# Moving turned q, k and x across partitions by DMA, for 64x64 tensor tiles in a fused attention and FFN kernel

## The chip, the cores and the metric

The kernel runs on one core of one Trainium2 chip. The metric is device time in microseconds (us) of one execution. Every kernel here was timed beside the kernel before on the same chip; most executions of the kernel before agree within 0.3%. A "fast" run is one no more than 1.5% above the fastest run of the same kernel; only fast runs enter a ratio. A ratio is the mean time of one kernel's fast runs over that of the other's of the same rounds, so it is not quite the ratio of the medians that are quoted.

Engine names in the profile: PE is TensorE (PEld its weight loads), DVE VectorE, ACT ScalarE, POOL GpSimd (here it only issues loads), SP SyncE (in the kernel before it only issues stores and two small loads at the start).

## The reference

Chunked attention over 64-token chunks, then an FFN without a nonlinearity:

```python
# q, k, v: (8, 8, 576, 64) float32
q_c = q.reshape(B, H, nc, 64, D)              # same for k, v
scores = scale * q_c @ k_c^T                  # 64 x 64 for each chunk and head
attn = softmax(scores)
out = attn @ v_c
x = out.transpose(0, 2, 1, 3).reshape(4608, 512)
return ((x @ w1) * (x @ w2)) @ w3 @ w_out     # d_ff = 1024
```

## The kernel before

Tokens are worked off in 18 "pairs" of 256 tokens (4 chunks). `ORDER` is a string that lists all steps in program order; each engine executes its own steps in that order. A letter is a step: T turns q or k of a pair (DVE transposes within blocks of 32x32), S scores, E exponential (ACT), P values, N normalise, X turns the result x (DVE), A and B the two FFN products, C copies the first to SBUF (ACT), M multiplies (DVE), O the output product, Y its copy. V, W and Z fold w3 and w_out into one matrix early on.

A DVE transpose leaves the 64 rows of the head dimension as two parts in the *same* 32 partitions. So scores contract over 32 partitions twice, and values write 32-partition tiles, which x then needs for its own transpose (shortened, `...` marks a cut):

```python
def do_S(p):                       # 64 matmuls a pair on 32x64 tiles
    ...
    for h in range(H):
        for e in range(2):
            for i in range(NB):
                mm(s_t[p][half[i % 2], i // 2, h * CH:(h + 1) * CH],
                   lhsT=qkT[blk[i], 1, e, h, :], rhs=qkT[blk[i], 0, e, h, :],
                   start=(e == 0), stop=(e == 1))

def do_P(p, u):                    # 64 matmuls a pair on 64x32 tiles
    ...
    mm(pv[blk[g], r, at:at + W],
       lhsT=e[half[r], u, 2 * g + n, qh * BL:(qh + 1) * BL],
       rhs=vbuf[p % 7][half[r], u, 2 * g + n, 0:W], start=True, stop=True)

def mm_ab(p, j, which):            # FFN: tiles of 256 tokens
    ...
    for i in range(2):
        for ki in range(KO):
            mm(ps_t[p, j][:, which, i * PT:(i + 1) * PT],
               lhsT=w[:, ki, (2 * j + i) * P:(2 * j + i + 1) * P],
               rhs=xt[:, ki, p * PT:(p + 1) * PT], start=(ki == 0), stop=(ki == KO - 1))

def do_O(p):                       # last pair: three pieces of one PSUM tile
    ...
    for u, n0, n1, copy in (...):
        mm_o(p, u, n0, n1)
        copy(o_sb[:, u, n0:n1], t[:, u, n0:n1])
        store(p, u, u + 1, n0, n1, o_sb)
```

The loads of q, k and v cast float32 to bf16 and go through POOL's queue; only q and k of pair 0 come through SP's queue and are cast by ACT. There are four PSUM tiles of 2 x 512 float32 for everything.

The softmax here doesn't subtract the row's maximum and nothing guards it: scores larger than these inputs give would overflow.

Of the kernel before, what the change touches and what calls it, by code (L numbers as in the profile page):

```python
# [9 lines left out]
l0 q1 i0 k1 v1 i1 i2 l2 i3 l3 l4 o h0 h1 l5 D0.0.16.64 T0.0 T0.1 l6 S0 T1.0 E0 P0 D0.1.4.512 T1.1 l7  # L10
N0.0 S1 D1.0.5.512 X0.0 N0.1 X0.1 A0.0 E1 B0.0 C0.0 P1 M0.0 A0.1 N1.0 X1.0 B0.1 C0.1 N1.1 A0.2 X1.1
B0.2 C0.2 M0.1 A1.0 T2.0 B1.0 C1.0 M0.2 A1.1 T2.1 l8 B1.1 C1.1 M1.0 S2 M1.1 A0.3 E2 T3.0 B0.3 C0.3
P2 M0.3 A1.2 N2.0 X2.0 B1.2 C1.2 N2.1 A1.3 X2.1 B1.3 C1.3 M1.2 A2.0 T3.1 l9 B2.0 C2.0 M1.3 S3 T4.0
A2.1 E3 M2.0 B2.1 T4.1 C2.1 P3 l10 M2.1 A2.2 N3.0 B2.2 C2.2 X3.0 A2.3 N3.1 B2.3 X3.1 C2.3 M2.2 S4
M2.3 A3.0 E4 B3.0 C3.0 A3.1 M3.0 B3.1 C3.1 V0 A3.2 M3.1 B3.2 C3.2 V1 A3.3 M3.2 B3.3 C3.3 V2 W0 M3.3
V3 T5.0 W1 Z0 V4 V5 T5.1 W2 Z1 V6 V7 T6.0 P4 l11 Z2 S5 T6.1 W3 E5 N4.0 X4.0 N4.1 X4.1 T7.0 A4.0 Z3
B4.0 T7.1 C4.0 P5 l12 M4.0 S6 N5.0 O0 E6 X5.0 N5.1 X5.1 T8.0 O1 Y0 T8.1 P6 l13 Y1 S7 N6.0 O2 E7 X6.0
N6.1 X6.1 T9.0 T9.1 O3 Y2 A4.1 Y3 B4.1 C4.1 A4.2 M4.1 B4.2 C4.2 A4.3 M4.2 B4.3 C4.3 P7 l14 M4.3 S8
N7.0 O4 E8 X7.0 N7.1 X7.1 T10.0 A5.0 T10.1 Y4 B5.0 C5.0 A5.1 M5.0 B5.1 C5.1 A5.2 M5.1 B5.2 C5.2 A5.3
M5.2 B5.3 C5.3 A6.0 M5.3 B6.0 C6.0 P8 l15 M6.0 S9 N8.0 O5 E9 X8.0 N8.1 X8.1 T11.0 A6.1 T11.1 Y5 B6.1  # L20
C6.1 A6.2 M6.1 B6.2 C6.2 A6.3 M6.2 B6.3 C6.3 P9 l16 M6.3 S10 N9.0 O6 E10 X9.0 N9.1 X9.1 T12.0 A7.0
T12.1 Y6 B7.0 C7.0 A7.1 M7.0 B7.1 C7.1 A7.2 M7.1 B7.2 C7.2 A7.3 M7.2 B7.3 C7.3 P10 l17 M7.3 S11
N10.0 O7 E11 X10.0 N10.1 X10.1 T13.0 A8.0 T13.1 Y7 B8.0 C8.0 A8.1 M8.0 B8.1 C8.1 A8.2 M8.1 B8.2 C8.2
A8.3 M8.2 B8.3 C8.3 P11 M8.3 S12 N11.0 O8 E12 X11.0 N11.1 X11.1 T14.0 A9.0 T14.1 Y8 B9.0 C9.0 A9.1
M9.0 B9.1 C9.1 A9.2 M9.1 B9.2 C9.2 A9.3 M9.2 B9.3 C9.3 P12 M9.3 S13 N12.0 O9 E13 X12.0 N12.1 X12.1
T15.0 A10.0 T15.1 Y9 B10.0 C10.0 A10.1 M10.0 B10.1 C10.1 A10.2 M10.1 B10.2 C10.2 A10.3 M10.2 B10.3
C10.3 P13 M10.3 S14 N13.0 O10 E14 X13.0 N13.1 X13.1 T16.0 A11.0 T16.1 Y10 B11.0 C11.0 A11.1 M11.0
B11.1 C11.1 A11.2 M11.1 B11.2 C11.2 A11.3 M11.2 B11.3 C11.3 P14 M11.3 S15 N14.0 O11 E15 X14.0 N14.1
X14.1 T17.0 A12.0 T17.1 Y11 B12.0 C12.0 A12.1 M12.0 B12.1 C12.1 A12.2 M12.1 B12.2 C12.2 A12.3 M12.2
B12.3 C12.3 P15 M12.3 S16 N15.0 O12 E16 X15.0 N15.1 X15.1 A13.0 Y12 B13.0 C13.0 A13.1 M13.0 B13.1  # L30
C13.1 A13.2 M13.1 B13.2 C13.2 A13.3 M13.2 B13.3 C13.3 P16 M13.3 S17 N16.0 O13 E17 X16.0 N16.1 X16.1
A14.0 Y13 B14.0 C14.0 A14.1 M14.0 B14.1 C14.1 A14.2 M14.1 B14.2 C14.2 A14.3 M14.2 B14.3 C14.3 P17
M14.3 A15.0 N17.0 X17.0 B15.0 C15.0 N17.1 O14 X17.1 M15.0 A15.1 Y14 B15.1 C15.1 A15.2 M15.1 B15.2
C15.2 A15.3 M15.2 B15.3 C15.3 A16.0 M15.3 B16.0 C16.0 O15 M16.0 A16.1 Y15 B16.1 C16.1 A16.2 M16.1
B16.2 C16.2 A16.3 M16.2 B16.3 C16.3 A17.0 M16.3 B17.0 C17.0 O16 M17.0 A17.1 Y16 B17.1 C17.1 A17.2
M17.1 B17.2 C17.2 A17.3 M17.2 B17.3 C17.3 M17.3 O17 Y17
# [4 lines left out]
def kernel(  # L41
# [24 lines left out]
    PT = 2 * UT  # L66
    NP = NT // PT
# [35 lines left out]
    xt = wpool.tile([P, KO, NT], bf, name="xt")  # L103
# [3 lines left out]
    vbuf = [consts.tile([P, 2, H, VW], bf, name=f"vbuf{i}") for i in range(7)]  # L107
# [16 lines left out]
    def load_qk(p, which=(0, 1)):  # L124
        if p not in qk_t:
            qk_t[p] = io.tile([P, 2, H, 2 * D], bf, tag="qk", bufs=6, name="qk")
        for s in which:
            if p == 0:

                raw = io.tile([P, H, 2 * D], f32, tag="raw", name="raw")  # L130
                inorder(nc.sync.dma_start(
                    raw[:], (q, k)[s][0, :, 0:4 * CH, :].rearrange("h (p t) d -> p h (t d)", t=2)))
                inorder(nc.scalar.copy(qk_t[p][:, s], raw[:]))  # L133
                continue
            for at, b, c, m in spans(4 * p, 4):
                load(qk_t[p][at * BL:(at + m) * BL, s],
                     (q, k)[s][b, :, c * CH:(c + m) * CH, :].rearrange("h (p t) d -> p h (t d)", t=2))

    def load_v(p):
        for u in range(2):  # L140
            for at, b, c, m in spans(4 * p + 2 * u, 2):
                load(vbuf[p % 7][at * CH:(at + m) * CH, u, :, 0:D],
                     v[b, :, c * CH:(c + m) * CH, :].rearrange("h p d -> p h d"))
# [17 lines left out]
    qkT_t, s_t, e_t, pv_t, xn_t = {}, {}, {}, {}, {}  # L161

    def do_T(p, s):


        if s == 0:
            qkT_t[p] = asb.tile([P, 2, 2, H, CH], bf, tag="qkT", bufs=2, name="qkT")
        inorder(nc.vector.transpose(  # L168
            qkT_t[p][:, s].rearrange("p e h (y t) -> p h t e y", t=2),
            qk_t[p][:, s].rearrange("p h (t e y) -> p h t e y", t=2, e=2)))  # L170

    def do_S(p):
        qkT = qkT_t.pop(p)
        s_t[p] = s_t.pop(p) if p in s_t else psum("s_ps")
        for h in range(H):
            for e in range(2):
                for i in range(NB):
                    mm(s_t[p][half[i % 2], i // 2, h * CH:(h + 1) * CH],
                       lhsT=qkT[blk[i], 1, e, h, :],
                       rhs=qkT[blk[i], 0, e, h, :], start=(e == 0), stop=(e == 1))  # L180
# [7 lines left out]
    def do_P(p, u):  # L188
        e = e_t[p] if u == 0 else e_t.pop(p)
        pv = pv_t[p, u] = psum("pv")  # L190
        for n in range(2):
            for qh in range(2):
                for g in range(NB):
                    for r in range(2):
                        at = (2 * qh + n) * W
                        mm(pv[blk[g], r, at:at + W],
                           lhsT=e[half[r], u, 2 * g + n, qh * BL:(qh + 1) * BL],
                           rhs=vbuf[p % 7][half[r], u, 2 * g + n, 0:W], start=True, stop=True)

    def do_P2(p):  # L200
        do_P(p, 0)
        do_P(p, 1)

    def do_N(p, u):
# [3 lines left out]
        xn_t[p, u] = asb.tile([P, 2, 4, D], bf, tag="xn", bufs=2, name="xn")  # L208
        inorder(nc.vector.tensor_mul(xn_t[p, u][:], pv[:, :, :, 0:D], rc.to_broadcast([P, 2, 4, D])))  # L209

    def do_X(p, u):
        t0 = p * PT + u * UT
        inorder(nc.vector.transpose(  # L213
            xt[:, :, t0:t0 + UT].rearrange("p o (m y) -> p m o y", y=BL),
            xn_t.pop((p, u))[:].rearrange("p r (c n) (z o) -> p (r c) o n z", c=2, o=KO)))

    ab_t, ps_t, a_t = {}, {}, {}
# [9 lines left out]
    def mm_ab(p, j, which):  # L227
        w = (w1, w2)[which]
        for i in range(2):
            for ki in range(KO):  # L230
                mm(ps_t[p, j][:, which, i * PT:(i + 1) * PT],
                   lhsT=w[:, ki, (2 * j + i) * P:(2 * j + i + 1) * P],
                   rhs=xt[:, ki, p * PT:(p + 1) * PT], start=(ki == 0), stop=(ki == KO - 1))

    def do_A(p, j):
        ps_t[p, j] = ps_t.pop((p, j)) if (p, j) in ps_t else psum("ab_ps")
        mm_ab(p, j, 0)

    def do_B(p, j):
        mm_ab(p, j, 1)  # L240
# [5 lines left out]
    def do_M(p, j):  # L246
        if p not in ab_t:
            ab_t[p] = msb.tile([P, FO, PT], bf, tag="ab", bufs=7, name="ab")
        inorder(nc.vector.tensor_mul(  # L249
            ab_t[p][:, 2 * j:2 * j + 2, :].rearrange("p j t -> p (j t)"), a_t.pop((p, j))[:],  # L250
            ps_t.pop((p, j))[:, 1, :]))

    def store(p, u0, u1, n0, n1, o_sb):
        inorder(nc.sync.dma_start(
            out[p * PT + u0 * UT:p * PT + u1 * UT, n0:n1].rearrange("(u p) n -> p u n", p=UT),
            o_sb[:, u0:u1, n0:n1]))

    def mm_o(p, u, n0, n1):
        for ki in range(FO):
            mm(ps_t[p][:, u, n0:n1], lhsT=ab_t[p][:, ki, u * UT:(u + 1) * UT],  # L260
               rhs=w3o[:, ki, n0:n1], start=(ki == 0), stop=(ki == FO - 1))

    def do_O(p):
        ps_t[p] = psum("o_ps")
        if p < NP - 1:
            for u in range(2):
                mm_o(p, u, 0, DM)
            del ab_t[p]
            return

        t = ps_t[p]
        o_sb = msb.tile([P, 2, DM], f32, tag="o_sb", name="o_sb")
        for u, n0, n1, copy in ((0, 0, DM, nc.scalar.copy), (1, 0, DM // 2, nc.scalar.copy),
                                (1, DM // 2, DM, nc.vector.tensor_copy)):
            mm_o(p, u, n0, n1)
            inorder(copy(o_sb[:, u, n0:n1], t[:, u, n0:n1]))  # L276
            store(p, u, u + 1, n0, n1, o_sb)

    def do_Y(p):
# [4 lines left out]
        store(p, 0, 2, 0, DM, o_sb)  # L284
# [29 lines left out]
    def load_half3(i):  # L314
# [7 lines left out]
    do = {"l": load_pair, "q": lambda p: load_qk(p, (0,)), "k": lambda p: load_qk(p, (1,)), "v": load_v, "i": load_w12, "o": load_wo, "h": load_half3, "T": do_T, "S": do_S, "E": do_E,  # L322
          "P": do_P2, "N": do_N, "X": do_X, "A": do_A, "B": do_B, "C": do_C, "M": do_M, "D": do_D, "V": do_V,
# [33 lines left out]
```

## Time and profile before

The median is 254.5 us; the profiled span is 252.7 us.

| what | value | where it is read |
|---|---|---|
| PE busy | 93% of the span | page, part 1 |
| one pair in the middle (152.10 to 164.10) | 12.0 us | windows |
| one pair late, with no attention left | 10.44 us (224.91 to 235.35) | timeline |
| values and scores of a pair | 0.63 + 0.64 us for 128 matmuls | timeline |
| loads keep DMA full (9 tenths or more) | until about 126 us | page, part 2 |

The page: PE's busy time, then busy tenths in 40 slices of 6.3 us for PE, the granted clock, and the DMA engines.

```profile
PE 234.9 (93%) x3841; PEld 170.5 (67%) x3841; DVE 156.4 (62%) x233; ACT 86.3 (34%) x116; POOL 82.9 (33%) x110
...
PE   1389999999899999999999999999999999999993
...
PEclk9999999999999999999999999999999999999999
DMA  7999999999999999999953020202021120102022
```

PE reads 9 nearly everywhere after the start, and so does DMA for the first 20 slices. The next view gives the busy time of each engine in three stretches (us and instruction count for PE, PEld, DVE, ACT, POOL, then the granted clock, a DMA share that counts overlapping packets, and GB/s).

```profile
73.00:130.00 57.00, 56.47 (x989) 39.57 (x988) 36.46 (x55) 20.47 (x27) 29.16 (x38) 1.00 1.58 182
152.10:164.10 12.00, 11.87 (x210) 8.96 (x209) 8.14 (x12) 4.38 (x6) 0.00 (x0) 1.00 0.13 47
225.00:235.50 10.50, 10.50 (x82) 7.84 (x81) 2.75 (x4) 3.36 (x5) 0.00 (x0) 1.00 0.13 51
```

PE has no idle time to speak of in any of them. The timeline of PE in one pair (start, length, operation, shapes, count):

```profile
152.10 0.70 PE L88 MATMUL pv<-vbuf,e 64*32 64x65 bf16 x64
152.73 0.70 PE L88 MATMUL s_ps<-qkT 32*64 32x64 bf16 x64
153.57 3.61 PE L88 MATMUL o_ps<-w3o,ab 128*128 128x512 bf16 x16
```

Start to start, values take 0.63 us, and from scores to the output product 0.84. (Elsewhere in this trace, where FFN products follow scores, scores take 0.64, as at 37.90 us.) The next view is the chain of waits for the same moment (start, length, what):

```profile
152.21 0.59 ACT a_sb L244
...
152.83 0.70 DVE ab L249
...
153.57 3.61 PE o_ps L88 x16
```

The chain does not run through values and scores. It runs through the copy of the last FFN product (ACT, 0.59 us) and its multiplication (DVE, 0.70), and the output product starts 0.04 us after the latter. Values and scores fill just that hole.

### The profile page before, as it was taken

How to read it: one execution, taken by the hardware profiler on the slowest of the kernel's cores; microseconds unless marked ns; L12 is line 12 of the kernel's file. 1: busy time of each engine (PE TensorE's matmuls, PEld its weight loads, DVE VectorE, ACT ScalarE, POOL GpSimd, SP SyncE). 2: the span in 40 equal slices, each digit the busy share in tenths (PEclk: the TensorE clock that was granted, in tenths of full speed). 3: DMA queues.
4: the chain of work that ended last, by engine and by line, in shares of the span. 5: the costliest groups of instructions: out<-in, count | busy, mean ns of one | idle time of the engine just before them, and what ended most of it. 6: DMA issues, size and time to landing. Idle time of an engine off the chain costs nothing.

```text
span 252.7 us, 8382 instructions
## 1 busy us (share of the span) xinstructions
PE 234.9 (93%) x3841; PEld 170.5 (67%) x3841; DVE 156.4 (62%) x233; ACT 86.3 (34%) x116; POOL 82.9 (33%) x110
## 2 busy tenths in 40 slices
PE   1389999999899999999999999999999999999993
PEld 1237878854555577866868686868686868678662
DVE  1665999699996457486665758584945445432230
ACT  3312424432433343333334243343334332323321
POOL 8756975657984567654020000000000000000000
PEclk9999999999999999999999999999999999999999
DMA  7999999999999999999953020202021120102022
GB/s 177 182 184 177 182 175 202 196 184 167 175 170 214 244 227 182 199 167 148 187 38 92 3 83 4 86 3 86 5 81 44 46 81 5 64 22 84 0 86 83
DMA packets 89763, 29.90 MB, mean 118 GB/s; under 512 B 73728, under 2 KB 85248, under 8 KB 89728
## 3 DMA queue, kind: packets, MB, share of 16 engines
q0 software_dynamic: 82592, 18.88, 80.4%
q1 hardware_dynamic: 7136, 10.49, 11.8%
q8 instruction: 30, 0.49, 0.7%
q14 instruction: 5, 0.04, 0.0%
HBM read 38.80 MB, written 9.44 MB: 191 GB/s over the span
## 4 chain that ended last, share of the span: by engine, by line
PE 65%; DMA 14%; DVE 10%; POOL 4%; ACT 3%; issue 3%; DVEq 0%; POOLq 0%
PE ab_ps L88 39%; PE o_ps L88 25%; DMA w<-in_moe_w_dram 4%; DVE ab L249 4%; DMA qk<-in_q_dram 4%; DMA qk<-in_k_dram 3%; DVE w3T L290 3%; DMA vbuf<-in_v_dram 3%; ACT a_sb L244 3%; POOL w L91 1%; DVE qkT L168 1%; POOL vbuf L91 1%; POOL qk L91 1%; POOL wo L91 1%; DVE xt L213 1%
## 5 line engine op out<-in xcount | busy, mean ns | idle before, releaser
L88 PE MATMUL ab_ps<-xt,w 128*128 128x256 bf16 x1136 | 128.0, 273 | 1.3 <-DVE xt L213 1.3
L88 PEld LDWEIGHTS <-w 128*128 128x128 bf16 x1152 | 112.3, 98 | 19.4 <-DVE xt L213 2.4
L249 DVE TENSOR_TENSOR ab<-a_sb,ab_ps 128x512 bf16<-128x512 f32 x71 | 48.3, 682 | 71.6 <-ACT a_sb L244 71.6
L244 ACT COPY a_sb<-ab_ps 128x512 f32<-128x512 f32 x71 | 41.6, 586 | 79.3 <-PE ab_ps L88 79.3
L88 PE MATMUL o_ps<-w3o,ab 128*128 128x512 bf16 (+1 forms) x296 | 65.3, 373 | 2.7 <-ACT o_sb L276 1.1
L88 PEld LDWEIGHTS <-ab 128*128 128x128 bf16 x296 | 28.7, 97 | 33.3 <-issue 1.6
L168 DVE STREAM_TRANSPOSE qkT<-qk 128x1024 bf16<-128x1024 bf16 x36 | 45.1, 1287 | 8.5 <-ACT qk L133 5.1
L91 POOL DMA_DIRECT2D vbuf<-in_v_dram x40 | 33.9, 852 | 31.3 <-PE pv L88 16.3
L283 ACT COPY o_sb<-o_ps 128x1024 f32<-128x1024 f32 x17 | 17.2, 1014 | 45.9 <-PE o_ps L88 43.2
L213 DVE STREAM_TRANSPOSE xt<-xn 128x512 bf16<-128x512 bf16 x36 | 25.6, 712 | 1.2
L209 DVE TENSOR_TENSOR xn<-pv,rc 128x512 bf16<-128x512 f32 x36 | 24.9, 692 | 1.2
L91 POOL DMA_DIRECT2D qk<-in_q_dram x23 | 18.1, 793 | 6.8 <-DMA qk<-in_k_dram 2.4
L184 ACT ACTIVATE e<-s_ps 128x1024 bf16<-128x1024 f32 x16 | 16.4, 1025 | 8.7 <-PE s_ps L88 8.4
L91 POOL DMA_DIRECT2D qk<-in_k_dram x23 | 18.0, 788 | 3.3 <-DMA w<-in_moe_w_dram 1.7
L88 PEld LDWEIGHTS <-qkT 32*64 32x64 bf16 x1152 | 11.4, 111 | 10.6 <-DVE qkT L168 9.6
L88 PE MATMUL w_ps<-wo,w3T 128*128 128x512 bf16 x64 | 14.2, 379 | 0.0
L88 PEld LDWEIGHTS <-e 64*32 64x32 bf16 x1152 | 10.1, 90 | 5.5 <-issue 3.6
L88 PE MATMUL pv<-vbuf,e 64*32 64x65 bf16 x1152 | 12.7, 197 | 1.1 <-ACT e L184 1.1
L91 POOL DMA_DIRECT2D w<-in_moe_w_dram x16 | 11.1, 697 | 5.4 <-DMA wo<-in_moe_w_out_dram 3.0
L88 PE MATMUL s_ps<-qkT 32*64 32x64 bf16 x1024 | 11.3, 193 | 0.0
L88 PEld LDWEIGHTS <-w3T 128*128 128x128 bf16 x64 | 6.2, 98 | 7.1
L290 DVE STREAM_TRANSPOSE w3T<-w 128x1024 bf16<-128x1024 bf16 x8 | 9.6, 1211 | 0.9 <-DMA w<-in_moe_w_dram 0.9
(20 smaller groups left out, 33.9 us busy)
## 6 DMA issues: line engine op xcount, KB each, us to landing
out_dram<-o_sb SPq DMA_DIRECT2D x17, 512.0 KB, 4.0
vbuf<-in_v_dram POOLq DMA_DIRECT2D x32, 128.0 KB, 6.7
w<-in_moe_w_dram POOLq DMA_DIRECT2D x16, 256.0 KB, 9.9
qk<-in_q_dram POOLq DMA_DIRECT2D x11, 256.0 KB, 6.6
qk<-in_k_dram POOLq DMA_DIRECT2D x11, 256.0 KB, 8.0
wo<-in_moe_w_out_dram POOLq DMA_DIRECT2D x4, 256.0 KB, 6.9
qk<-in_q_dram POOLq DMA_DIRECT2D x4, 192.0 KB, 9.4
qk<-in_k_dram POOLq DMA_DIRECT2D x4, 192.0 KB, 8.7
```

The lines of the kernel that those rows point to most:

```text
L88: return inorder(nc.tensor.matmul(*a, **kw))
L91: return inorder(nc.gpsimd.dma_start(dst, src))
L168: inorder(nc.vector.transpose(qkT_t[p][:, s].rearrange("p e h (y t) -> p h t e y", t=2), qk_t[p][:, s].rearrange("p h (t e y) -> p h t e y ...
L184: inorder(nc.scalar.activation(e_t[p][:].rearrange("p u h q -> p u (h q)"), s_t.pop(p)[:], Exp, scale=scale, bias=0.0))
L209: inorder(nc.vector.tensor_mul(xn_t[p, u][:], pv[:, :, :, 0:D], rc.to_broadcast([P, 2, 4, D])))
L213: inorder(nc.vector.transpose(xt[:, :, t0:t0 + UT].rearrange("p o (m y) -> p m o y", y=BL), xn_t.pop((p, u))[:].rearrange("p r (c n) (z o) ...
L244: inorder(nc.scalar.copy(a_t[p, j][:], ps_t[p, j][:, 0, :]))
L249: inorder(nc.vector.tensor_mul(ab_t[p][:, 2 * j:2 * j + 2, :].rearrange("p j t -> p (j t)"), a_t.pop((p, j))[:], ps_t.pop((p, j))[:, 1, :]))
L283: inorder(nc.scalar.copy(o_sb[:], ps_t.pop(p)[:]))
L290: inorder(nc.vector.transpose(w3T_t[f][:].rearrange("p k (f y) -> p f k y", y=BL), w3[:, NB * f:NB * (f + 1), :].rearrange("p f (k x) -> p ...
```

## The change

The intent: from pair 6 on, feed PE with larger tiles. DMA moves (SBUF to SBUF, issued from SP) carry the second part of each turned q and k to the partitions beside the first, so that scores contract over 64 partitions in one matmul; values write 64-partition tiles; x is moved after its turn instead. Scores and values then take 32 matmuls a pair each instead of 64. FFN tiles take 512 tokens (two pairs). The last output gets three PSUM tiles. The whole `ORDER` is new: attention of later pairs comes earlier, and all loads go through POOL in a new order. Six groups of two pairs are moved, 1 MB of q,k (step G) and 0.5 MB of x (step H) each: 96 moves, 9.4 MB. The main pieces, shortened:

```diff
+    def do_G(g, a):                               # q,k of two pairs change partitions
+        for i in (2 * a, 2 * a + 1):
+            for e in range(2):
+                move(qkm_t[g][blk[2 * a + e], i % 2], qkT_t[g][blk[i], e])   # nc.sync.dma_start
...
     def do_S(p):
+                for i in (0, 3, 1, 2):            # p >= 6
                     mm(s_t[p][half[i % 2], i // 2, h * CH:(h + 1) * CH],
+                       lhsT=qkm_t[g][half[i // 2], i % 2, m, 1, h, :],
+                       rhs=qkm_t[g][half[i // 2], i % 2, m, 0, h, :], start=True, stop=True)
...
     def do_P(p):
+                    for g, r in ((0, 0), (1, 1), (1, 0), (0, 1)):          # p >= 6
+                        mm(pv[half[g], r, m * W:(m + 1) * W], lhsT=e[half[r], u, 4 * g + m, :],
+                           rhs=vbuf[p % 6][half[r], u, 4 * g + m, 0:W], start=True, stop=True)
...
+    def do_H(g, a):                               # x of two pairs changes partitions
+        for k_ in range(2):
+            for i in (2 * a, 2 * a + 1):
+                move(xt[blk[2 * a + k_], i % 2], xm_t[g][blk[i], k_].rearrange("p o m t -> p (o m t)"))
...
-            qk_t[p] = io.tile([P, 2, H, 2 * D], bf, tag="qk", bufs=6, name="qk")
+            qk_t[p] = io.tile([P, 2, H, 2 * D], bf, tag="qk", bufs=5, name="qk")
...
     def do_O(p):                                  # last pair
+            t = psum("o_ps")
+            mm_o(t[:, 0, 0:n1 - n0], p, u, n0, n1)
+            inorder(copy(o_sb[:, u, n0:n1], t[:, 0, 0:n1 - n0]))
...
     ORDER: (rewritten; its end)
-B17.1 C17.1 A17.2 M17.1 B17.2 C17.2 A17.3 M17.2 B17.3 C17.3 M17.3 O17 Y17
+A16.7 M16.6 B16.7 C16.7 O11 M16.7 O12 ... O16 Y15 Q15 O17 Y16 Q16 Y17 Q17
```

## The prediction

> **What bounds the kernel now.** TensorE. The page shows PE busy 93% of a 252.7 us span, at a granted clock of 0.99 or more in all slices. In the timeline, from the first FFN matmul (18.26 us) on, idle time is only a few us. From about 93 us a pair takes 12.0 us (152.10 to 164.10), with 11.87 us of PE busy in the windows view: values 0.63, scores 0.64, output 3.6, both FFN products 7.0. A pair late in the run, with no attention left, takes 10.44 us. So attention costs 1.55 us a pair: 128 tiny matmuls at 9.8 ns each (1.27 us), the rest probably switches between tile shapes. DMA is the second limit: until 131 us its slices read 9, at 160 to 218 GB/s; DVE is busy 62%.
>
> **What the change removes.**
> 1. Small matmuls for pairs 6 to 17: 64 to 32 per pair for scores and for values, with the moving sizes kept (64 and 65 columns). Both old shapes cost 9.8 ns a matmul though one uses 4 tiles and the other 8, so the limit looks like issue, not the tile: a score tile turned over in 40 ns. The Trainium skill (TensorEngine Tiling, "Available Configurations") gives 64x64 four independent tiles; 8 uses of each at 40 ns give 0.32 us. Estimate 0.35 instead of 0.64: 0.6 us a pair, 7 us in all.
> 2. FFN tiles of 512 tokens: 256-column matmuls cost 109.4 ns each (7.0/64), the 512-column ones of the output 215.6 (3.45/16): 0.2 us per two pairs, 1.2 us.
> 3. Tail: PE's waits for the copy of the shared output tile (1.1 us) go, and the last outputs no longer wait for the last product (about 0.9 us): 2 us.
> 4. Start: all loads by the software queue in a new order. The first FFN product should start at 15 to 16 us instead of 18.3, but its second weight slice comes later (after pair 2's loads), so PE stands about where it was at 22 us. Gain about 0.
>
> **What it adds.** About 9 MB of moves inside the core: 6 groups of 1 MB for q,k and 0.5 MB for x. Stores of 10.49 MB took 11.8% of 16 engines' span, about 2.9 us per MB; so 9 MB is some 25 us of DMA, of which 3 to 4 MB (10 us) falls while loads saturate DMA. The Trainium skill (DMA: Bandwidth & Descriptors, "Issuing engines are not separate DMA queues") says they share the same 16 engines; in this trace loads slow when stores begin. Each move's 2 to 4 us latency is hidden, since the order moves several us of PE work ahead of its use. Load-bound stalls: DVE executes in order, so a turn waiting for a late q or k (pairs 13 to 15), or for w3 near 49 us, holds up products and then PE. Estimate 4 us lost.
>
> **Sum.** All of the PE savings are critical: -7 -1.2 -2 +4 gives -6 to -7: predicted 247.5 us, 80% range 243.5 to 253. Faster by over 2%: 0.70; within 2%: 0.26; slower: 0.04.
>
> **Right or wrong would show as:** 64x64 scores and values at 0.3 to 0.4 us per pair in the timeline (0.6 would mean a per-tile limit, and the gain falls to 3 us); FFN matmuls at 215 ns; no PE waits in the last 8 us; DMA share high until about 140 us; PE waits on DVE turns between 45 and 120 us summing to about 4 us; PE busy near 225 us.
>
> **What would make it wrong:** moves slowing the loads far more than stores did, so that DVE and PE starve between 70 and 120 us (255 us possible); stores queued behind waiting moves on the in-order SP queue; no stalls at all (243 us).

## The result, and the profile after

The kernel after is correct and slower: 266.79 us median of four runs (264.27 to 267.87), ratio 1.047 (95% interval 1.039 to 1.055). The prediction had 247.5 us with a range up to 253. The page of the kernel after, same rows (slices are 6.6 us here):

```profile
PE 234.1 (88%) x2713; PEld 131.0 (49%) x2728; DVE 152.4 (57%) x232; ACT 82.9 (31%) x114; POOL 84.4 (32%) x112
...
PE   4477989999996999756949999999999999999992
...
PEclk9999999999999799997997999999999999999999
DMA  8999999999999999999999520166015003002344
```

PE's busy time is hardly lower than before (234.1 us for 234.9), although it has 29% fewer matmuls (2713 for 3841); its share fell from 93% to 88%. The digits show holes near 80 us, from 106 to 126 and near 133, and the granted clock drops to 7 in the slices that follow. DMA stays full until about 146 us instead of 126. PE's waits (who waited for what: total us, times, longest):

```profile
PE s_ps L92 <- DMA qkm<-qkT: 11.3, 3, 4.6
...
PE ab_ps L92 <- ACT o_sb L336: 2.2, 1, 2.2
```

Three waits of scores for moved q,k take 11.3 us. The wait of 2.2 us is for a slow store: the copy that PE waits for had itself waited 7.97 us for a store that reads its buffer (ACT's timeline, at 112.51). The windows view of the same stretch that before had 56.47 us of PE work in 57:

```profile
73.00:130.00 57.00, 46.87 (x640) 27.40 (x643) 40.81 (x60) 17.97 (x23) 27.34 (x35) 0.94 1.67 219
```

It has 46.87 busy, part of it at a lower clock. The timeline of PE around the first and second long wait (the bracket is the idle time before, and what ended it):

```profile
81.86 1.91 PE L92 MATMUL ab_ps<-xt,w 128*128 128x256 bf16 x16
83.70 0.21 PE L92 MATMUL s_ps<-qkm 64*64 64x64 bf16 x1
86.94 0.93 PE L92 MATMUL s_ps<-qkm 64*64 64x64 bf16 x63 [3.03 <-DMA qkm<-qkT]
87.81 3.06 PE L92 MATMUL ab_ps<-xt,w 128*128 128x256 bf16 x16
...
121.97 1.08 PE L92 MATMUL s_ps<-qkm 64*64 64x64 bf16 x63 [4.63 <-DMA qkm<-qkT]
122.98 3.35 PE L92 MATMUL ab_ps<-xt,w 128*128 128x512 bf16 x8
```

Each stall is followed by slow work: 16 FFN matmuls of 256 columns take 3.06 us after the first, against 1.91 before it; 8 of 512 columns take 3.35 after the second, against 1.90 in the lines shown further down. The windows view shows why (granted clock is the third number from the right):

```profile
84.00:87.00 3.00, 0.06 (x1) 0.09 (x1) 0.07 (x1) 0.39 (x1) 0.68 (x1) 1.00 1.94 161
88.00:91.00 3.00, 3.00 (x32) 1.95 (x34) 2.02 (x3) 1.71 (x3) 2.07 (x3) 0.57 1.24 308
```

During the stall the clock reads 1.00, and 0.57 once work is back. The Trainium skill (TensorE: Matmul & The Clock Gate, "What's actually happening", with its table of the two states) says that an idle window of about 3.4 us halves the clock and that a busy one restores it; the trace agrees in kind. The length of a stall alone does not decide it, though: in the kernel c4_nov (below) a stall of 3.16 us was followed by work at full clock (1.00), and one of 1.90 us by a clock of 0.54. Over the three stalls of the kernel after the slow clock cost 1.2, 1.5 and 1.0 us on the FFN groups alone, which the prediction did not have.

What the change did for PE itself is what was predicted. In the quiet stage two pairs of scores stand next to each other, and values take 0.38 us start to start:

```profile
156.84 0.71 PE L92 MATMUL s_ps<-qkm 64*64 64x64 bf16 x64
157.48 1.90 PE L92 MATMUL ab_ps<-xt,w 128*128 128x512 bf16 x8
159.31 0.45 PE L92 MATMUL pv<-vbuf,e 64*64 64x65 bf16 x32
159.69 5.35 PE L92 MATMUL ab_ps<-xt,w 128*128 128x512 bf16 x24
```

Scores cost 0.64 us for two pairs and values 0.38 us a pair, so 0.7 us a pair for both where the kernel before takes 1.27.

The DMA view gives out<-in, queue, count, KB each and the median us from issue to landing. The kernel after while loads run (73 to 135 us):

```profile
qkm<-qkT SPq DMA_DIRECT2D x32, 128.0 KB, 7.8
...
qk<-in_k_dram POOLq DMA_DIRECT2D x4, 256.0 KB, 14.3
...
qk<-in_q_dram POOLq DMA_DIRECT2D x2, 192.0 KB, 17.7
```

The same kernel when no loads run (155 to 200 us):

```profile
qkm<-qkT SPq DMA_DIRECT2D x8, 128.0 KB, 2.4
```

The same 128 KB move lands in 7.8 us beside the loads and in 2.4 us without them. The loads suffer too: see the kernel without moves below.

Finally the end. ACT's timeline in the last 7 us:

```profile
259.05 0.58 ACT L329 COPY o_sb<-o_ps 128x512 f32<-128x512 f32 x1 [4.17 <-PE o_ps L92]
259.88 0.37 ACT L329 COPY o_sb<-o_ps 128x256 f32<-128x256 f32 x1 [0.24 <-PE o_ps L92]
260.15 1.02 ACT L336 COPY o_sb<-o_ps 128x1024 f32<-128x1024 f32 x1
```

The copy of pair 16 (the line at 260.15) stands behind the copies of pair 17 in program order, so a 512 KB store starts last. From PE's last matmul to the end it takes 5.0 us (260.73 to 265.7), against 3.3 before.

### The profile page after: what moved, and what is told of

It reads as the page before. It is cut to its first block, busy times and chain, and to the rows that moved or that the text cites. A ratio compares the mean times of both kernels' runs of the same rounds, so it can differ in the third digit from the quotient of the medians.

```text
span 265.7 us, 6328 instructions
## 1 busy us (share of the span) xinstructions
PE 234.1 (88%) x2713; PEld 131.0 (49%) x2728; DVE 152.4 (57%) x232; ACT 82.9 (31%) x114; POOL 84.4 (32%) x112
## 3 DMA queue, kind: packets, MB, share of 16 engines
HBM read 38.80 MB, written 9.44 MB: 182 GB/s over the span
## 4 chain that ended last, share of the span: by engine, by line
PE 60%; DMA 22%; DVE 7%; POOL 3%; issue 2%; SPq 2%; ACT 1%; DVEq 0%; POOLq 0%
PE ab_ps L92 39%; PE o_ps L92 17%; DMA qkm<-qkT 9%; DMA out_dram<-o_sb 6%; DMA w<-in_moe_w_dram 5%; DVE qkT L171 2%; DMA xt<-xm 2%; SPq L163 2%; PE s_ps L92 2%; DVE w3T L347 2%; POOL qk L95 1%; PE pv L92 1%; POOL vbuf L95 1%; PE w_ps L92 1%; DVE xn L229 1%
## 5 line engine op out<-in xcount | busy, mean ns | idle before, releaser
L92 PE MATMUL ab_ps<-xt,w 128*128 128x512 bf16 (+1 forms) x752 | 132.0, 333 | 4.6 <-ACT o_sb L336 2.2
L92 PEld LDWEIGHTS <-w 128*128 128x128 bf16 x768 | 75.2, 100 | 57.1 <-issue 7.3
L92 PE MATMUL o_ps<-w3o,ab 128*128 128x512 bf16 (+1 forms) x285 | 63.1, 373 | 0.6
L95 POOL DMA_DIRECT2D vbuf<-in_v_dram x40 | 33.8, 854 | 25.5 <-DMA qk<-in_q_dram 10.1
L336 ACT COPY o_sb<-o_ps 128x1024 f32<-128x1024 f32 x17 | 17.2, 1012 | 45.3 <-PE o_ps L92 33.8
L95 POOL DMA_DIRECT2D qk<-in_q_dram x24 | 19.0, 792 | 10.5 <-issue 2.0
L95 POOL DMA_DIRECT2D qk<-in_k_dram x24 | 18.9, 789 | 7.5 <-DMA vbuf<-in_v_dram 3.7
L249 DVE STREAM_TRANSPOSE xm<-xn 128x512 bf16<-128x512 bf16 x24 | 16.1, 694 | 0.2
L92 PE MATMUL s_ps<-qkm 64*64 64x64 bf16 x384 | 6.2, 204 | 11.3 <-DMA qkm<-qkT 11.3
L92 PEld LDWEIGHTS <-qkm 64*64 64x64 bf16 x384 | 5.1, 117 | 14.0 <-DMA qkm<-qkT 8.4
L92 PE MATMUL pv<-vbuf,e 64*32 64x65 bf16 (+1 forms) x768 | 9.8, 200 | 2.3 <-ACT e L201 2.3
L92 PEld LDWEIGHTS <-e 64*32 64x32 bf16 (+1 forms) x768 | 7.6, 101 | 8.5 <-issue 5.4
```

The lines of the kernel that those rows point to most:

```text
L92: return inorder(nc.tensor.matmul(*a, **kw))
L95: return inorder(nc.gpsimd.dma_start(dst, src))
L249: inorder(nc.vector.transpose(xm_t[g][:, u, :, m].rearrange("p o (c y) -> p c o y", y=BL), xn_t[p][:].rearrange("p u r m d -> p (u r) m d" ...
L336: inorder(nc.scalar.copy(o_sb[:], ps_t.pop(p)[:]))
```

## The experiments

Eighteen kernels ran besides these two. Their diffs are shortened to the lines that make the difference. "Wrong" means that the numbers computed are wrong but the work is of the same shape.

| kernel | median us | what it is |
|---|---|---|
| before | 254.5 | |
| after | 266.79 | |
| a1_nomove | 248.29 | after, no moves at all (wrong) |
| a2_unread | 269.47 (one fast run: 265.0) | after, moves made but not read (wrong) |
| a3_noturn | 258.20 | after, small tiles, no moves |
| a4_from12 | 255.61 | after, moves from pair 12 on |
| b1_unread_nowar | 269.26 | a2 with one more source buffer (wrong) |
| b2_stores_act | 270.65 | after, stores on ACT's queue |
| b3_xonly | 255.05 | after, only x moved |
| b4_qkonly | 266.84 | after, only q,k moved |
| c1_quiet12 | 257.94 | order of before, moves from pair 12 on |
| c2_tail | 253.14 | before, last output in 3 PSUM tiles |
| c3_quiet_nomove | 252.44 | c1 without moves |
| c4_nov | 262.02 | after, v loads of pairs 12 to 17 left out (wrong) |
| d1_half | 251.94 | b1, half the q,k bytes (wrong) |
| d2_spread | 264.17 | b1, q,k bytes over all partitions (wrong) |
| d3_hybrid | 251.19 | new order, moves late |
| d4_hybrid_nomove | 253.94 | d3 without moves |
| d5_hybrid2 | 248.41 | d3 with DVE's turns spread |
| d6_qk14 | 253.49 | after, q,k moved from pair 14 on, x from 6 |

The theories at the start: A, scores wait for moves that land late. B, moves take DMA time from the loads, so q and k come late. C, the new order loses the time by itself.

### No moves, and moves that nobody reads

```diff
 # a1_nomove
     def do_G(g, a):
+        return                       # same in do_H
-                       lhsT=qkm_t[g][half[i // 2], i % 2, m, 1, h, :],
+                       lhsT=qkT_t[g][half[i // 2], i % 2, m, 1, h, :],
-            rhs = new_xt(p // 2)[:].rearrange(...)
+            rhs = xm_t[p // 2][:].rearrange(...)
 # both: 2 buffers of xt and 4 of xm instead of 4 and 2
 # a2_unread: the same reads, but do_G and do_H still move
```

> All 96 partition moves left out; scores and FFN read the unmoved tiles (wrong result on purpose, same work elsewhere). Theory A (the matmuls wait for moves that land in 8 us while loads keep DMA full): PE waits of 11.3 us on the moved q,k vanish, as do the half-clock stretches after them; 246 to 250 us. Theory C (the new load order and program order lose the time by themselves): stays at 258 us or above.

Measured: 248.29 us, ratio 0.975 (0.973 to 0.977). Theory C falls: with all other parts of the change in place, the order and the tiles are faster than before. The moves cost 266.79 - 248.29 = 18.5 us.

> All moves are made but nothing reads their results (wrong result on purpose). Theory A (waiting for the landing): close to the kernel without moves, within 3 us, about 250 us. Theory B (moves take DMA time from the loads, so q, k and v come late): at least 6 us above the kernel without moves, 256 us or more, with DVE waits on loads of q. If stores behind moves on the SP queue matter, a PE wait on the output copy of about 2 us stays.

Measured: 265.0 us in its one fast run; the other three, 269.1 to 270.2, count as slow by the 1.5% rule. Theory A as stated falls: nobody waits for a landing, and the time is as bad. But the trace left a second suspect, since DVE's turns waited 8.0 us until moves had read their source (two buffers). So this was taken away:

```diff
 # b1_unread_nowar = a2_unread and
-tag="qkT", bufs=2
+tag="qkT", bufs=3
-tag="qkm", bufs=2
+tag="qkm", bufs=1
```

> As the kernel whose moves nobody reads (269.5), but with three buffers for the turned q,k, so that DVE's turns no longer wait until a move has read its source (8.0 us of DVE waits there); one buffer for the moved q,k; wrong result on purpose. Theory B (moves and loads slow each other on the DMA engines): still 262 us or more, the waits on late loads of q stay. Theory W (turns wait for their source buffer): falls to 256 us or below.

Measured: 269.26 us (268.39 to 269.75). Its waits, PE first, then DVE:

```profile
PE ab_ps L92 <- DVE ab L318: 8.3, 2, 6.9
PE pv L92 <- DVE ab L318: 4.5, 1, 4.5
```

```profile
DVE qkT L172 <- DMA qk<-in_q_dram: 23.1, 6, 7.4
...
DVE qkT L172 <- DMA qk<-in_k_dram: 5.8, 3, 3.4
```

This is theory B at work. DVE waits 23.1 us for q loads (8.9 in the kernel without moves). DVE executes in order, so a product step M stands behind a turn T that waits for a load, and PE waits for that M (12.8 us in these two lines). The longest case, first DVE's timeline, then PE's:

```profile
132.84 1.30 DVE L172 STREAM_TRANSPOSE qkT<-qk 128x1024 bf16<-128x1024 bf16 x1 [7.42 <-DMA qk<-in_q_dram]
134.05 0.65 DVE L318 TENSOR_TENSOR ab<-a_sb,ab_ps 128x512 bf16<-128x512 f32 x1
```

```profile
134.75 5.01 PE L92 MATMUL ab_ps<-xm,w 128*128 128x512 bf16 x16 [6.86 <-DVE ab L318]
```

The turn waits 7.42 us for q, the product follows it at once, and PE, idle for 6.86 us, starts 0.05 us after the product's end. The same stretch, windows view, of the kernel without moves:

```profile
73.00:130.00 57.00, 56.08 (x826) 31.75 (x825) 51.83 (x80) 23.88 (x33) 30.14 (x38) 1.00 1.62 171
```

PE is full there. And the landing of the loads without moves, from 73 to 135 us:

```profile
qk<-in_k_dram POOLq DMA_DIRECT2D x4, 256.0 KB, 7.9
qk<-in_q_dram POOLq DMA_DIRECT2D x2, 192.0 KB, 7.8
```

A 192 KB load of q takes 7.8 us without moves and 17.7 with them; one of 256 KB of k 7.9 and 14.3. The last v loads are issued at 119.77 us without moves and at 132.56 with them (POOL's timeline, first the kernel without moves, then the kernel after):

```profile
119.77 1.76 POOL L95 DMA_DIRECT2D vbuf<-in_v_dram  x2 [3.23 <-PE pv L92]
```

```profile
132.56 1.75 POOL L95 DMA_DIRECT2D vbuf<-in_v_dram  x2 [1.51 <-PE pv L92]
```

So loads and moves slow each other. In the kernel after the moved q,k arrive last and scores wait; when nobody reads them, the loads arrive last and DVE waits. Either path alone is long enough. In the kernel after, DVE's turns also waited 8.7 us for moves to read their source; the third buffer was tried only where nobody reads the moves, so what it would bring there is not known.

### Old tiles, and moves from pair 12 on, in the order of the kernel after

```diff
 # a3_noturn: threshold 6 -> 18 for S, P, X, G, H (512-token FFN tiles stay from pair 6)
 # a4_from12: threshold 6 -> 12
-            if p < 6:
+            if p < MV:
```

> The kernel after with its order, loads, 512-token FFN tiles and tail, but scores and values of all pairs on the old small tiles, no moves; correct. Theory A: small tiles cost 0.55 us a pair more for 12 pairs (about 7 us) than the kernel without moves: 253 to 257 us. Theory C: 262 us or more.

Measured: 258.20 us, correct, ratio 1.010 (fast runs 257.0 to 258.6, mean 257.8). A little above the expected range. One more run was slow (262.2). Its trace shows PE "issue" waits inside small-tile scores and values, and DVE turns waiting for scores (4.1 us), because q,k buffers are now held until scores have read them; so it is a control with some waits of its own.

> Moves and 64x64 tiles only from pair 12 on; correct. Theory A: two of the three long waits (pairs 6 and 10) go, the one of pair 12 near 136 us may stay since loads still run: 252 to 258 us. Theory B: loads of the middle stage are no longer slowed, same number. Theory C: 262 us or more.

Measured: 255.61 us, ratio 1.002 (0.997 to 1.007), as expected. Fewer moves beside loads, less loss; no gain either.

### The queue, and which moves

```diff
 # b2_stores_act: output stores
-        move(out[...], o_sb)                          # nc.sync.dma_start
+        inorder(nc.scalar.dma_start(out[...], o_sb))
 # b3_xonly: do_S and do_G use threshold 18; P, X, H keep 6
 # b4_qkonly: do_S and do_G keep 6; P, X, H use 18
```

> The kernel after with the output stores issued from ScalarE's queue, so that moves and stores no longer stand behind each other on SP; correct. Theory Q (one in-order queue for moves and stores costs the time): 260 us or below. Theory B: within 3 us of the kernel after, 264 to 268 us; landing of moves stays near 8 us in the load stage.

Measured: 270.65 us, ratio 1.062, above both expected ranges. Another queue does not help; PE waited 14.6 us for moved q,k. The Trainium skill (DMA: Bandwidth & Descriptors, "Issuing engines are not separate DMA queues") says that all issuing engines share the same 16 DMA engines, and this run agrees.

> Only values on 64x64 tiles, only x moved (3 MB); scores as before; correct. Against the kernel with no moves and small tiles (258.2): values save 0.25 us on 12 pairs, 3 us; theory B with a cost in proportion to bytes adds a third of 21 us, 7 us: 259 to 264 us.

> Only scores on 64x64 tiles, only q and k moved (6 MB); values as before; correct. Scores save 0.3 us on 12 pairs, 3.5 us; theory B in proportion to bytes adds two thirds of 21 us, 14 us: 265 to 271 us. If only what scores wait for counted (theory A), about the same, so this run tells the share of q,k from that of x, not A from B.

Measured: x alone 255.05 us (2.7 below the fast runs of a3_noturn, near the 3 us expected for values on large tiles, so moved x costs nothing that shows), q,k alone 266.84. A cost in proportion to bytes would have put x at 259 to 264; it missed. The expectation for q,k held. q,k is twice the bytes, more of it moves while loads run, and its users stand closer behind it.

### Fewer loads, fewer bytes, other partitions

```diff
 # c4_nov: after, with
     def load_v(p):
+        if p >= 12:
+            return
 # d1_half: b1_unread_nowar, with rows of 2 KB
-move(qkm_t[g][blk[2 * a + e], i % 2], qkT_t[g][blk[i], e])
+move(qkm_t[g][blk[2 * a + e], i % 2, 0], qkT_t[g][blk[i], e, 0])
 # d2_spread: b1_unread_nowar, 128 KB a move as 1 KB rows on 128 partitions
+move(qkm_t[g][:, i % 2, e, a], qkT_t[g][:, e, i % 2, a])
```

> The kernel after with its moves, but no loads of v for pairs 12 to 17 (1.5 MB of loads in the stage where moves of pairs 8 to 13 run; values of these pairs use old v, wrong result on purpose). Theory B: the later two PE waits on moved q,k (4.6 and 3.6 us) shrink by half or more, 256 to 262 us. If the moves' own landing time were the cause whatever the loads do: within 3 us of the kernel after.

Measured: 262.02 us, ratio 1.031. Taking 1.5 MB of *loads* away makes the moves' user faster by 4.8 us: the third wait on moved q,k fell from 3.6 to 1.9 us, the second only from 4.6 to 4.2. The time is at the upper edge of what was expected; the second wait is not what was expected: the moves for it were still issued beside loads of q and k, and landed in 8.6 us.

> The kernel with moves that nobody reads and no wait for their source (269.3; 248.3 without moves), each q,k move halved to 2 KB rows, 3 MB instead of 6; wrong result on purpose. If the bytes moved beside the loads set the loss: between 255 and 262 us. If the count of moves sets it: 267 us or more.

Measured: 251.94 us, ratio 0.990. Half the q,k bytes bring back 17 of the 21 us, more than expected (the rows are halved with them, the count of moves is not). With 0, 3 and 6 MB of q,k moves (the latter two with 3 MB of x) the unread series reads 248.3, 251.9 and 269.3 us: the loads have slack for the first megabytes, and past it the loss is steep.

> The same kernel, each q,k move with its full 128 KB but as 1 KB rows on all 128 partitions, no change of partition; wrong result on purpose. If the bytes set the loss whatever their form: 265 to 272 us. If the 32-partition form does: 258 us or below.

Measured: 264.17 us, just below the range for "bytes" and far from "form". Some 16 of the 21 us stay when the same bytes keep their partitions. The remaining 5 us can be the form or the row size, which also changed; no run tells which. The profile pages show that the spread moves also took less DMA time: packets of the queue of moves and stores were busy 60.9 us of all 16 engines here (23.1% of 263.7) and 67.8 in b1 (25.3% of 268.0).

### Moves where no loads run

c1 keeps loads, start and order of the kernel before up to pair 11, and moves only pairs 12 to 17. c3 is the same without moves; c2 is the tail alone.

```diff
 # c1_quiet12, ORDER of before with
+... T13.0 A8.0 T13.1 G6.0 G6.1 ... P11 M8.3 S12 ...
+... T15.0 A10.0 T15.1 G7.0 G7.1 ... P13 M10.3 S14 ...
 # and 512-token FFN tiles from pair 12, Y16 ahead of O17
 # c3_quiet_nomove: threshold for S, P, X, G, H = 18
 # c2_tail: before, with a PSUM tile for each piece of the last output
```

> The loads, start and program order of the kernel before up to pair 11; moves, 64x64 tiles and 512-token FFN tiles only for pairs 12 to 17, after the loads have ended; last output in 3 PSUM tiles with the store of pair 16 ahead of it; correct. Theory B (moves are cheap where no loads run): 0.6 us a pair for 6 pairs, 0.6 us for the FFN, 2 us at the tail against 254.5: 247.5 to 250 us, no PE wait on moved q,k. If moves cost as much in the quiet stage: 253 us or more.

> The kernel before with the last output in 3 PSUM tiles alone; correct. The two PE waits on the copies (1.1 us) go: 253.3 to 253.8 us. If the copies or stores bound the end: 254.5.

> The same order as the kernel with moves from pair 12, but small tiles for all pairs and no moves; 512-token FFN tiles from pair 12 and the new tail stay; correct. 251 to 253 us; the difference to it is what 64x64 tiles with moves earn in the quiet stage, 3.6 us expected.

Measured: c1 257.94 us (ratio 1.013), c2 253.14 (0.995, a gain of 1.3 us, just over what was expected), c3 252.44 (0.992). So c1's moves lost 5.5 us where 3.6 of gain were expected, with hardly any loads left: theory B is not all. PE's timeline of c1:

```profile
154.32 0.46 PE L90 MATMUL s_ps<-qkm 64*64 64x64 bf16 x32
155.51 3.61 PE L90 MATMUL o_ps<-w3o,ab 128*128 128x512 bf16 x16 [0.73 <-DVE ab L321]
...
166.32 0.19 PE L90 MATMUL s_ps<-qkm 64*64 64x64 bf16 x1
167.91 0.67 PE L90 MATMUL s_ps<-qkm 64*64 64x64 bf16 x31 [1.41 <-DMA qkm<-qkT]
```

Two things show. First, scores of pair 14 wait 1.41 us for a move that was issued only just before: the eight moves of a group take about 5 us to issue on SP and then 2.4 to land, and this order leaves less. Second, the output product waits 0.73 us for DVE's multiplication after the faster scores. This is the hole of the chain of waits shown for the kernel before: copy and multiplication take 1.3 us, values and scores used to fill it, and now they end early. This pair still takes 12.0 us (154.04 to 166.04), so in this order smaller attention buys nothing. c1 changes both things at once; that each counts is read from the trace, not from a run.

The hybrid order therefore takes S of two pairs together, between FFN steps, with P after further FFN steps (the pattern that the kernel after uses from 156 us on), and at least 8 us between G and S:

```diff
 # d3_hybrid: ORDER of before up to "P11 M8.3", T13.1 followed by G6, then
+... A9.1 M9.0 B9.1 C9.1 S12 M9.1 S13 E12 A9.2 T15.0 B9.2 E13 C9.2 P12 A9.3 ...
+... A12.7 M12.6 B12.7 C12.7 O10 M12.7 O11 ... S16 S17 E16 A14.0 B14.0 E17 C14.0 P16 ...
 # 64x64 tiles and moves from pair 12, 512-token FFN tiles from pair 10
 # d4_hybrid_nomove: the same with threshold 18
 # d5_hybrid2: d3 with T15.1, T16 and T17 moved to FFN steps without other DVE work
-X14.1 P15 T17.0 T17.1 G8.0 G8.1 A12.4 M12.3
+A12.0 T17.0 B12.0 E15 C12.0 P14 A12.1 M12.0 T17.1 G8.0 G8.1 B12.1
```

> Loads, start and order of the kernel before up to pair 11, then moves, 64x64 tiles for pairs 12 to 17 and 512-token FFN tiles from pair 10, with at least 8 us of PE work between each group of moves and its use, scores of two pairs next to each other; tail as in the quiet-stage kernel; correct. If distance was the cause of its loss: no PE wait on moved q,k and 247 to 250 us, which beats both kernels. If moves cost by themselves in the quiet stage: 253 us or more.

> The hybrid order with small tiles for all pairs and no moves; correct. 251 to 253 us; moves with 64x64 tiles should earn 3 to 4 us over it.

> The hybrid kernel (251.2) with the turns of pairs 15 to 17 spread over FFN steps that have no other VectorE work; correct. The two PE waits on VectorE (2.0 us) go: 249 to 250.5 us. If these waits only hid behind others: 251 us.

Measured: d3 251.19 us (0.987), d4 253.94 (0.997), d5 248.41 (0.976, 0.974 to 0.977). d3 and d4 were above their ranges, and moves with 64x64 tiles earned 2.8 us (d4 less d3) where 3 to 4 were expected. In d3 PE had no wait for moved q,k, but two waits of 2.0 us together for M behind two turns in a row. d5 took these away and, 2.8 us faster than d3, came in below its range. d5 is correct and beats both kernels: 2.4% below the kernel before, 18 us below the kernel after. PE's timeline over one group of two pairs:

```profile
170.11 0.71 PE L90 MATMUL s_ps<-qkm 64*64 64x64 bf16 x64
171.02 1.89 PE L90 MATMUL ab_ps<-xt,w 128*128 128x512 bf16 x8 [0.20 <-issue]
172.84 0.45 PE L90 MATMUL pv<-vbuf,e 64*64 64x65 bf16 x32
...
185.79 7.07 PE L90 MATMUL o_ps<-w3o,ab 128*128 128x512 bf16 x31
192.79 0.71 PE L90 MATMUL s_ps<-qkm 64*64 64x64 bf16 x64
```

A group takes 22.68 us (170.11 to 192.79) where two pairs took 24.0, and nothing waits for a move or for M. A control of d5's own order without moves was not run; d4, that of d3, is 5.5 us slower than d5.

```diff
 # d6_qk14: after, S and G from pair 14 on, P, X, H from 6
```

> The kernel after with x moved from pair 6 on but q and k moved and scores on 64x64 tiles only from pair 14 on, when the loads have ended; correct. Against x alone (255.05) 4 pairs save 0.3 us each: 253 to 255 us, no PE wait on moved q,k. If q,k moves cost in any stage: 257 us or more.

Measured: 253.49 us, ratio 0.995, no wait for moved q,k; against x alone 4 pairs saved 1.6 us (1.2 expected). So q,k moves pay also in the order of the kernel after, once the loads have ended.

## Why the prediction was wrong, point by point

- *"TensorE bounds the kernel now."* Right. DMA was named as second limit, and it is where the time went.
- *Small matmuls, 7 us.* Right as a cost on PE: 0.35 us a pair expected for scores and for values each, 0.32 and 0.38 measured. Whether it is gained depends on the order: without moves, the new order gains it (a1 is 9.5 us below the fast runs of a3, which has some waits of its own), while in the order of the kernel before the saving falls into the hole before the output product (c1). The prediction took 1.55 us a pair as the cost of attention from the difference of two pair times and did not read the chain of waits beside it.
- *512-token FFN tiles, 1.2 us.* Right: 215.8 ns a matmul (13.81 us for 64 in the chain of the kernel after).
- *Tail, 2 us.* Half right. The three PSUM tiles gain 1.3 us alone (c2), but the new order puts the copy of pair 16 behind those of pair 17, and 1.7 us are lost at the end.
- *Start, about 0.* Somewhat off: the first FFN product began at 17.65 us, not 15 to 16. In the kernel without moves the work that the kernel before has done at 71.6 us is done at about 74.1 (75.19, less 1.75 us for a unit that it is ahead, plus 0.64 for scores that it is behind): 2.5 us late.
- *"Estimate 4 us lost"* to moves and loads. **This is the step that failed.** It measured 18.5 us. Four parts of it were off:
  - *Cost of a megabyte.* 2.9 us of DMA was taken over from the stores. In the same measure (packet time on all 16 engines, from the profile pages) the moves took 4.3 us per MB in the kernel after, and 4.4 where few loads run (c1 against c3). So all moves are 41 us of DMA and not 25.
  - *Amount beside the loads.* Some 5 MB (four groups of q,k and two of x issued by 132 us) and not 3 to 4: an estimate of 22 us of DMA (5 x 4.3) and not 10. It was assumed that slack would take most of it; the last loads were issued 12.8 us later (a rough measure, since these issues also wait for a buffer that PE frees).
  - *"Each move's 2 to 4 us latency is hidden".* Moved q,k landed in 7.8 us beside the loads, and scores waited 11.3 us for them. The path that was predicted, late loads that hold up turns, products and then PE, does not show in the kernel after, where PE has no wait on DVE from 45 us on; it shows where nobody reads the moves (b1).
  - *The slow clock* after each stall, 3.7 us on the FFN alone, was not thought of.

  On PE the waits for moved q,k, the wait for a slow store and the slow clock make 11.3 + 2.2 + 3.7 = 17.2 us. The list of what could go wrong did name loads slowed so that PE starves between 70 and 120 us, and stores behind moves.
- The total without the failed term, 247.5 - 4 = 243.5, would still have been 4.8 us under the 248.3 of the kernel without moves; start and tail make up most of that.

What stays open: how the DMA engines divide their time between loads and moves. The Trainium skill (DMA: Bandwidth & Descriptors, "Queues, rings and completion order") says that each engine takes turns between queues packet by packet, which would fit large move rows holding up small load rows; no run here shows it directly. Also open is the kernel after with a third buffer for the turned q,k.

## What to carry to other kernels

A DMA move inside the core is not free because PE is the bottleneck: before adding one, count its DMA time by what moves themselves take (here 4.3 us per MB, more than stores), look whether loads keep the DMA engines full at that time, and put it where they don't, with issue time plus landing time (here 5 + 2.4 us) of other work before its use. When a saving is costed from a busy time, look at the chain of waits at the same moment: work that fills a hole in another chain saves nothing until the order is changed too. The kernel with nothing changed but the suspected cost left out, wrong numbers and all, is the first experiment to make; and one in which the cost stays but nobody waits for it is the second.

## What the Trainium skill lacked or had wrong

- DMA: Bandwidth & Descriptors: its fit for one DMA ("Anatomy of one DMA", 2.0 us plus bytes over 436e3, measured on the other issue path) gives an estimate of 2.3 us for 128 KB, and moves in the quiet stage landed in 2.4. It has no figure for a transfer beside a saturated casting load stream: the same move landed in 7.8 us there, and 192 KB loads went from 7.8 to 17.7 us.
- DMA: Bandwidth & Descriptors: no measured DMA time of moves between the partitions of one core's SBUF, only a ceiling for their bandwidth. Here the moves' queue was busy 40.9 us of all 16 engines for 9.44 MB (25.0% of 265.7 us with moves, 10.3% of 247.4 without), 4.3 us per MB, against 2.7 for stores of the same size in all (25.5 us for 9.44 MB).
- TensorEngine Tiling (Array Packing), "Instruction Overhead", gives about 60 cycles of overhead a matmul. Side by side on several tiles 64 matmuls of 64 columns started within 0.64 us, 10 ns each, on 32x64, 64x32 and 64x64 tiles alike (12 ns for values on 64x64); this page has no figure for this rate (the gap is this page's alone; the skill has figures for starts on neighbouring tiles elsewhere).
- TensorE: Matmul & The Clock Gate: its table of the two states gives an idle window of about 3.4 us for the slow state. Here shorter stalls were enough, and their length alone did not decide: 3.03 us in the kernel after was followed by a clock of 0.57 (about 1 us after work had resumed, and not during the stall, 1.00), 1.90 us in c4_nov by 0.54, but 3.16 us in c4_nov by 1.00.
